# Score products over all 128 rows of the array, keys masked per head, in one core's gated-attention training kernel

## The chip, the cores and the metric

The kernel runs on one core of one Trainium2 chip. The metric is the device time of one execution in microseconds (us); lower is better. One profiled execution gives a trace with every instruction of the engines: PE (TensorE matmul), PEld (TensorE weight load), DVE (VectorE), ACT (ScalarE), POOL (GpSimd) and SP (SyncE, here only a DMA queue). "PEclk" is the TensorE clock that was granted, as a share of full speed; this trace has only the values 0.50 and 1.00 in it, and means between them for longer stretches.

## The reference, cut to what matters

The program computes a gated mix of two attention blocks and all its gradients. Part A is the one that is changed: multi-query attention with 32 query heads of 18 dimensions, one key and one value head, 2048 tokens, no mask.

```
q = (x @ wq).reshape(B, S, 32, 18)          # S = 2048
k = x @ wk ;  v = x @ wv                    # one head of 18
scores = einsum('bhqd,bkd->bhqk', q, k) * 18 ** -0.5
p = softmax(scores) ;  o = einsum('bhqk,bkd->bhqd', p, v)
a = o.reshape(B, S, 32 * 18) @ wo
out = sigmoid(x . gate_w) * a + (1 - sigmoid(x . gate_w)) * b
# reference(): out and its gradients by jax.vjp
```

Part B (`b`, a memory-augmented recurrent attention) and its gradients take the rest of the time and are not touched.

## The kernel before

Part A stands first in the program. `a_setup` loads x and the weights, projects keys and values and writes the queries and the output gradients to memory. `a_attention` is the long part, and the one that the change edits. `a_final` makes the weight gradients. Then Part B runs.

`a_attention` goes over 8 groups of 4 heads. A group's 128 partitions hold 4 heads of 32 rows each; of the 32, 18 are the head's dimensions and one carries an offset, so that 19 are used. `kaug` and `vaugT` hold the one key and value head, repeated for the four places. A group begins with `tr16`, which transposes tiles of 128x128 on PE: two calls make `qtok` and `doT`, and a third, between the two loops, makes `doaT`.

Each group then runs two loops of 4 blocks with 16 iterations each, so 512 iterations of each loop over all groups:

- Loop 1 (for a block of 512 queries, over 16 key tiles) makes the output and the query gradient.
- Loop 2 (for a block of 512 keys, over 16 query tiles) makes the key and value gradients.

An iteration treats the four heads as two pairs. For a pair it computes the scores `s` (two matmuls), the gradient products `d` (two matmuls), the exponential `E = exp(s)` on ACT and `U = d * E` on DVE. E and U then go as moving operand into accumulating matmuls: in loop 1 with `evA`/`evB` (64 columns of the array) and `ku` (32 columns), in loop 2 with `dog` and `qtok` (32 columns each). The matmuls of a pair lie at different row groups (`s`, `d`) or column groups (the others) of the array, given by `tp`, and two that stand next to each other in the instruction order run at the same time. In this text such a stream of 512 columns, of one matmul or of several at the same time, is called a slot.

The two tiles of two PSUM banks, `s` and `d`, come from one pool tag `a_w` of three buffers; the two accumulators take the other two of the eight banks. Instruction order on each engine is set when the program is built, by a scheduler that works from these dependences and buffers; each engine runs its list in order.

In rows of the profile and of the instruction order all matmuls stand at line 66 (`mm`) or 71 (`tr`), so they are told apart by their tiles: `a_w<-a_qaug,a_kaug` is a score product, `a_w<-a_doT,a_vaugT` a gradient product of loop 1 (`a_vaugT,a_doaT` of loop 2), `a_acc<-...` an accumulation. A shape such as `19*128 19x512` means 19 active rows, 128 active columns, and a moving operand of 19 partitions by 512.

Of the kernel before, what the change touches and what calls it, by code (L numbers as in the profile page):

```python
# [6 lines left out]
ACT = mybir.ActivationFunctionType  # L7
ALU = mybir.AluOpType
AX = mybir.AxisListType
BF16 = mybir.dt.bfloat16  # L10
F32 = mybir.dt.float32
P = 128
# [17 lines left out]
class Kern:  # L30
# [1055 lines left out]
    def a_attention(self, keep, sp, pacc, ps):  # L1086


        nc = self.nc
# [5 lines left out]

        def tr16(src_fn, dst):
            for t4 in range(0, NTT, 8):
                pt = ps.tile([P, 8, P], BF16, name="a_w", bufs=3)
                for t in range(8):
                    self.tr(pt[:, t, :], src_fn(t4 + t), P)  # L1100
                self.evac(dst[:, t4 * P:(t4 + 8) * P], pt[:].rearrange("p t c -> p (t c)"))

        for g in range(8):
            qaug = sp.tile([P, T], BF16, name="a_qaug", bufs=2)
# [4 lines left out]
            tr16(lambda t: qaug[:, t * P:(t + 1) * P], qtok)  # L1109
            doT = sp.tile([P, T], BF16, name="a_doT", bufs=1)  # L1110
            tr16(lambda t: dog[:, t, :], doT)
            srows = [slice(32 * i, 32 * i + 19) for i in range(4)]
            for qb in range(T // 512):
                qs = slice(qb * 512, qb * 512 + 512)
                acc = [pacc.tile([P, 512], F32, name=f"a_acc{b}", bufs=1) for b in range(2)]
                for kt in range(NTT):
                    ks = slice(kt * P, (kt + 1) * P)
                    Es, Us = [], []
                    for pr in range(2):
                        s = ps.tile([P, 2, 512], F32, name="a_w", bufs=3)  # L1120
                        for j in range(2):
                            r = srows[2 * pr + j]
                            self.mm(s[:, j, :], lhsT=self.kaug[r, ks], rhs=qaug[r, qs], tp=(r.start, 0))
                        d = ps.tile([P, 2, 512], F32, name="a_w", bufs=3)
                        for j in range(2):
                            r = srows[2 * pr + j]
                            self.mm(d[:, j, :], lhsT=self.vaugT[r, ks], rhs=doT[r, qs], tp=(r.start, 0))
                        ex = sp.tile([P, 2, 512], BF16, name="a_E", bufs=4)
                        nc.scalar.activation(ex[:], s[:], ACT.Exp, scale=SCALEA)  # L1129
                        u = sp.tile([P, 2, 512], BF16, name="a_U", bufs=4)  # L1130
                        nc.vector.tensor_tensor(out=u[:], in0=d[:], in1=ex[:], op=ALU.mult)  # L1131
                        Es.append(ex)
                        Us.append(u)
                    for pr in range(2):
                        ev = self.evA if pr == 0 else self.evB
                        for j in range(2):
                            self.mm(acc[pr][64 * j:64 * j + 64, :], lhsT=ev[:, kt, :], rhs=Es[pr][:, j, :],
                                    start=(kt == 0), stop=False, tp=(0, 64 * j))
                    for pr in range(2):
                        for j in range(2):  # L1140
                            b = 64 * j + (32 if pr == 0 else 0)
                            self.mm(acc[pr][b:b + 32, :], lhsT=self.ku[:, kt, :], rhs=Us[pr][:, j, :],
                                    start=False, stop=(kt == NTT - 1), tp=(0, b))
                accs = sp.tile([P, 2, 512], F32, name="a_accs", bufs=1)
                nc.scalar.copy(accs[:, 0, :], acc[0][:, :])
                nc.vector.tensor_copy(accs[:, 1, :], acc[1][:, :])
                pt = ps.tile([P, 2, 4, P], F32, name="a_w", bufs=3)
                for b in range(2):
                    for t in range(4):
                        nc.tensor.transpose(pt[:, b, t, :], accs[:, b, t * P:(t + 1) * P], self.identF[:])  # L1150
                tk = sp.tile([P, 2, 4, P], F32, name="a_tk", bufs=1)
                nc.scalar.copy(tk[:], pt[:])
                ts = slice(qb * 4, qb * 4 + 4)
                for b in range(2):
                    v = tk[:, b].rearrange("p t (j c) -> p t j c", c=64)
                    o0, k1, k2, u0 = (0, 19, 32, 37) if b == 0 else (32, 51, 0, 5)
                    h0 = 4 * g + 2 * b
                    osl = self.otok[:, ts, h0 * DA:(h0 + 2) * DA].rearrange("p t (j e) -> p t j e", e=DA)
                    qsl = self.dqtok[:, ts, h0 * DA:(h0 + 2) * DA].rearrange("p t (j e) -> p t j e", e=DA)
                    dsl = dog[:, ts, 64 * b:64 * b + 64].rearrange("p t (j c) -> p t j c", c=32)  # L1160
                    rl = sp.tile([P, 4, 2, 1], F32, name="a_rl", bufs=2)
                    nc.vector.reciprocal(rl[:], v[:, :, :, o0 + 18:o0 + 19])
                    nc.gpsimd.tensor_tensor(out=osl, in0=v[:, :, :, o0:o0 + DA], in1=rl[:].to_broadcast([P, 4, 2, DA]),
                                            op=ALU.mult)
                    prod = sp.tile([P, 4, 2, DA], F32, name="a_prod", bufs=2)
                    nc.gpsimd.tensor_tensor(out=prod[:], in0=osl, in1=dsl[:, :, :, 0:DA], op=ALU.mult)
                    dd = sp.tile([P, 4, 2, 1], F32, name="a_dd", bufs=2)
                    nc.vector.tensor_reduce(out=dd[:], in_=prod[:], axis=AX.X, op=ALU.add)
                    m1 = sp.tile([P, 4, 2, DA], F32, name="a_m1", bufs=2)
                    nc.gpsimd.tensor_tensor(out=m1[:, :, :, 0:13], in0=v[:, :, :, k1:k1 + 13],  # L1170
                                            in1=dd[:].to_broadcast([P, 4, 2, 13]), op=ALU.mult)
                    nc.gpsimd.tensor_tensor(out=m1[:, :, :, 13:18], in0=v[:, :, :, k2:k2 + 5],
                                            in1=dd[:].to_broadcast([P, 4, 2, 5]), op=ALU.mult)
                    nc.gpsimd.tensor_tensor(out=m1[:], in0=v[:, :, :, u0:u0 + DA], in1=m1[:], op=ALU.subtract)
                    nc.gpsimd.tensor_tensor(out=dsl[:, :, :, 0:DA], in0=dsl[:, :, :, 0:DA],
                                            in1=rl[:].to_broadcast([P, 4, 2, DA]), op=ALU.mult)
                    nc.vector.scalar_tensor_tensor(out=dsl[:, :, :, DA:DA + 1].rearrange("p t j c -> p t (j c)"),
                                                   in0=dd[:].rearrange("p t j c -> p t (j c)"), scalar=-1.0,
                                                   in1=rl[:].rearrange("p t j c -> p t (j c)"),
                                                   op0=ALU.mult, op1=ALU.mult)  # L1180
                    rls = sp.tile([P, 4, 2, 1], F32, name="a_rls", bufs=2)
                    nc.gpsimd.tensor_scalar(out=rls[:], in0=rl[:], scalar1=SCALEA, scalar2=None, op0=ALU.mult)
                    nc.gpsimd.tensor_tensor(out=qsl, in0=m1[:], in1=rls[:].to_broadcast([P, 4, 2, DA]), op=ALU.mult)
            doaT = sp.tile([P, T], BF16, name="a_doaT", bufs=1)
            tr16(lambda t: dog[:, t, :], doaT)
            for kb in range(T // 512):
                ks = slice(kb * 512, kb * 512 + 512)
                acc = [pacc.tile([P, 512], F32, name=f"a_acc{b}", bufs=1) for b in range(2)]
                for qt in range(NTT):
                    qs = slice(qt * P, (qt + 1) * P)  # L1190
                    Es, Us = [], []
                    for pr in range(2):
                        s = ps.tile([P, 2, 512], F32, name="a_w", bufs=3)
                        for j in range(2):
                            r = srows[2 * pr + j]
                            self.mm(s[:, j, :], lhsT=qaug[r, qs], rhs=self.kaug[r, ks], tp=(r.start, 0))
                        d = ps.tile([P, 2, 512], F32, name="a_w", bufs=3)
                        for j in range(2):
                            r = srows[2 * pr + j]
                            self.mm(d[:, j, :], lhsT=doaT[r, qs], rhs=self.vaugT[r, ks], tp=(r.start, 0))  # L1200
                        ex = sp.tile([P, 2, 512], BF16, name="a_E", bufs=4)
                        nc.scalar.activation(ex[:], s[:], ACT.Exp, scale=SCALEA)  # L1202
                        u = sp.tile([P, 2, 512], BF16, name="a_U", bufs=4)
                        nc.vector.tensor_tensor(out=u[:], in0=d[:], in1=ex[:], op=ALU.mult)  # L1204
                        Es.append(ex)
                        Us.append(u)
                    for b, src, lt in ((0, Es, lambda i: dog[:, qt, 32 * i:32 * i + 32]),
                                       (1, Us, lambda i: qtok[:, qt * P + 32 * i:qt * P + 32 * i + 32])):
                        for i in range(4):
# [223 lines left out]
```

## Time and profile before

| what | value |
|---|---|
| median of 3 runs | 11707.12 us (11702.79 to 11712.66) |
| the profiled execution | 11713.39 us, span of its instructions 11711.6 us |
| PE busy | 10959.3 us, 94% of the span |
| DVE, ACT, POOL busy | 4411.1, 3615.3, 1254.4 us |
| mean granted TensorE clock | 0.722 |
| `a_attention` (first transposition to last accumulation) | 184.45 to 5053.34 us |

The profile cuts the span into 40 equal slices of 293 us; `a_attention` fills slices 1 to 17. Where matmuls are pipelined, a PE that is "busy" need not run at its peak, and at a granted clock of 0.50 the same column count takes twice the time, which counts as busy too. So PE's row has to be read together with the row of the clock.

### The profile page before, as it was taken

To read this page: it belongs to the slowest core of one execution; us is meant where nothing else is said; L and a number is where in the kernel's file an instruction comes from. 1 tells how busy PE (TensorE), PEld (TensorE's weight loads), DVE (VectorE), ACT (ScalarE), POOL (GpSimd) and SP (SyncE) were. 2 spreads that over 40 slices of the span, in tenths; PEclk is the share of its full clock that TensorE was granted. 3 is DMA by queue.
4 is the path that set the end of the run, shared out by engine and by line. 5 is a ranking of instruction groups with operands and counts; after the bars stand their busy time and mean duration, and the time that the engine had idled before them with its cause. 6 is when DMAs were issued, how large, how long until landed. Compare 5 with 4: busy or idle time off the path is not lost. (4 is left out here: it accounts for less than half of the span.)

```text
span 11711.6 us, 208963 instructions
## 1 busy us (share of the span) xinstructions
PE 10959.3 (94%) x91222; PEld 4451.6 (38%) x91222; DVE 4411.1 (38%) x6054; ACT 3615.3 (31%) x4858; POOL 1254.4 (11%) x2894
## 2 busy tenths in 40 slices
PE   7999999999999999989989998888879998999799
PEld 2212121212121212134445555555546665555444
DVE  4555555555555555534422223333322222111200
ACT  3444444444444444423311112222211111111100
POOL 3000000000000000013300002222210000111200
PEclk7555555555555555579989997777779998777799
DMA  2000000000000000035521114444442224666644
GB/s 67 1 4 1 4 1 4 1 4 1 1 4 1 4 1 1 1 116 234 218 82 49 51 49 164 161 155 155 158 164 78 79 78 137 189 189 185 205 144 146
DMA packets 550248, 961.27 MB, mean 82 GB/s; under 512 B 183433, under 2 KB 361746, under 8 KB 529170
## 3 DMA queue, kind: packets, MB, share of 16 engines
q1 hardware_dynamic: 482850, 693.21, 18.5%
q0 software_dynamic: 65168, 253.37, 5.7%
q8 instruction: 713, 11.68, 0.4%
q14 instruction: 205, 1.68, 0.0%
q10 hardware_dynamic: 1312, 1.33, 0.0%
HBM read 543.67 MB, written 404.03 MB: 81 GB/s over the span
## 5 line engine op out<-in xcount | busy, mean ns | idle before, releaser
L1204 DVE TENSOR_TENSOR a_U<-a_w,a_E 128x1024 bf16<-128x1024 f32 x1024 | 1252.0, 1224 | 1131.6 <-ACT a_E L1202 1088.3
L1131 DVE TENSOR_TENSOR a_U<-a_w,a_E 128x1024 bf16<-128x1024 f32 x1024 | 1253.5, 1225 | 964.7 <-ACT a_E L1129 964.7
L1202 ACT ACTIVATE a_E<-a_w 128x1024 bf16<-128x1024 f32 x1024 | 1048.6, 1024 | 1376.8 <-PE a_w L66 1375.5
L1129 ACT ACTIVATE a_E<-a_w 128x1024 bf16<-128x1024 f32 x1024 | 1047.9, 1024 | 1182.7 <-PE a_w L66 1182.7
L66 PE MATMUL a_w<-a_kaug,a_qaug 19*128 19x512 bf16 x2048 | 902.5, 601 | 4.1 <-ACT a_E L1202 3.4
L66 PE MATMUL a_w<-a_vaugT,a_doaT 19*128 19x512 bf16 x2048 | 836.7, 621 | 20.5 <-DVE a_U L1204 14.7
L66 PE MATMUL a_acc<-a_E,a_dog 128*32 128x512 bf16 x2048 | 626.1, 602 | 71.4
L66 PE MATMUL a_w<-a_doT,a_vaugT 19*128 19x512 bf16 x2048 | 671.7, 624 | 4.9 <-ACT a_E L1129 3.8
L66 PE MATMUL a_w<-a_qaug,a_kaug 19*128 19x512 bf16 x2048 | 659.1, 600 | 3.7 <-ACT a_doT L63 3.2
L66 PE MATMUL a_acc<-a_U,a_ku 128*32 128x512 bf16 x2048 | 626.2, 608 | 0.0
L66 PE MATMUL a_acc<-a_U,a_qtok 128*32 128x512 bf16 x2048 | 623.8, 607 | 0.6 <-DVE a_U L1204 0.6
L66 PE MATMUL w_acc<-w_col,w_h 128*128 128x512 bf16 (+1 forms) x2400 | 526.3, 381 | 11.3 <-DMA w_col<-dqx 11.3
L66 PEld LDWEIGHTS <-d_g 128*32 128x32 bf16 x18432 | 498.8, 97 | 30.1 <-issue 11.1
L66 PEld LDWEIGHTS <-a_qaug 19*128 19x128 bf16 x2048 | 152.2, 98 | 655.5 <-issue 655.5
L61 DVE CAST p_tok<-p_pb 128x512 bf16<-128x512 f32 x384 | 265.3, 692 | 318.6 <-PE p_pb L66 318.6
L66 PE MATMUL a_acc<-a_E,a_evB 128*64 128x512 bf16 x1024 | 326.5, 613 | 53.6 <-ACT a_E L1129 0.6
L66 PEld LDWEIGHTS <-a_dog 128*32 128x32 bf16 x2048 | 109.4, 101 | 652.6 <-issue 652.4
L66 PEld LDWEIGHTS <-w_h 128*128 128x128 bf16 (+1 forms) x2400 | 237.5, 101 | 300.3 <-issue 35.1
L66 PEld LDWEIGHTS <-a_ku 128*32 128x32 bf16 x2048 | 105.3, 101 | 640.6 <-issue 640.6
L66 PEld LDWEIGHTS <-a_qtok 128*32 128x32 bf16 x2048 | 107.8, 101 | 623.8 <-issue 623.4
L63 ACT COPY p_em<-p_tr 128x512 bf16<-128x512 bf16 x384 | 225.1, 586 | 357.9 <-PE p_tr L71 356.4
L66 PE MATMUL a_acc<-a_E,a_evA 128*64 128x512 bf16 x1024 | 325.2, 633 | 0.0
(484 smaller groups left out, 15185.9 us busy)
## 6 DMA issues: line engine op xcount, KB each, us to landing
xt_k<-p_tok SPq DMA_DIRECT2D x16, 1024.0 KB, 3.9
xe_k<-p_em POOLq DMA_DIRECT2D x16, 1024.0 KB, 5.3
xs_k<-p_seg POOLq DMA_DIRECT2D x64, 256.0 KB, 3.6
xt_v<-p_tok SPq DMA_DIRECT2D x16, 1024.0 KB, 4.3
xe_v<-p_em POOLq DMA_DIRECT2D x16, 1024.0 KB, 5.7
xs_v<-p_seg POOLq DMA_DIRECT2D x64, 256.0 KB, 3.7
xt_q<-p_tok SPq DMA_DIRECT2D x16, 1024.0 KB, 4.3
xe_q<-p_em POOLq DMA_DIRECT2D x16, 1024.0 KB, 5.7
```

The lines of the kernel that those rows point to most:

```text
L61: nc.vector.tensor_copy(out, in_)
L63: nc.scalar.copy(out, in_)
L66: return self.nc.tensor.matmul(out, lhsT, rhs, start=start, stop=stop, tile_position=tp, skip_group_check=True)
L1129: nc.scalar.activation(ex[:], s[:], ACT.Exp, scale=SCALEA)
L1131: nc.vector.tensor_tensor(out=u[:], in0=d[:], in1=ex[:], op=ALU.mult)
L1202: nc.scalar.activation(ex[:], s[:], ACT.Exp, scale=SCALEA)
L1204: nc.vector.tensor_tensor(out=u[:], in0=d[:], in1=ex[:], op=ALU.mult)
```

## The change

The change edits `a_attention` alone. The score product of a head no longer uses the head's own 32 rows, but all 128: the queries (all four heads of the group) stand against `kmask`, a copy of the keys with one slice per head in which the rows of the other three heads are zero. `kmask` is filled at the start of `a_attention`: a memset on POOL and four copies on DVE. The score matmul has no row group any more (no `tp`), so two of them can't run at the same time. The gradient products keep their row groups, but now take 32 rows instead of 19 (the rest are zero). Scores go to tiles of one bank (`a_s`, two buffers) and their exponential is made per head, in two instructions of 512 instead of one of 1024. The gradient products keep two banks (`a_d`, two buffers). Together that is again six banks.

```diff
+        srows = [slice(32 * i, 32 * i + 32) for i in range(4)]
+        kmask = keep.tile([P, 4, T], BF16, name="a_kmask")
+        nc.gpsimd.memset(kmask[:], 0.0)
+        for i in range(4):
+            nc.vector.tensor_copy(kmask[srows[i], i, :], self.kaug[srows[i], :])
+
+        def pair(pr, sl, sr, dl, dr):
+
+            d = ps.tile([P, 2, 512], F32, name="a_d", bufs=2)
+            ex = sp.tile([P, 2, 512], BF16, name="a_E", bufs=4)
+            for j in range(2):
+                s = ps.tile([P, 512], F32, name="a_s", bufs=2)
+                self.mm(s[:, :], lhsT=sl(2 * pr + j), rhs=sr(2 * pr + j))
+                nc.scalar.activation(ex[:, j, :], s[:, :], ACT.Exp, scale=SCALEA)
+            for j in range(2):
+                r = srows[2 * pr + j]
+                self.mm(d[:, j, :], lhsT=dl(r), rhs=dr(r), tp=(r.start, 0))
+            u = sp.tile([P, 2, 512], BF16, name="a_U", bufs=4)
+            nc.vector.tensor_tensor(out=u[:], in0=d[:], in1=ex[:], op=ALU.mult)
+            return ex, u
...
-            srows = [slice(32 * i, 32 * i + 19) for i in range(4)]
...
-                    for pr in range(2):
-                        s = ps.tile([P, 2, 512], F32, name="a_w", bufs=3)
-                        for j in range(2):
-                            r = srows[2 * pr + j]
-                            self.mm(s[:, j, :], lhsT=self.kaug[r, ks], rhs=qaug[r, qs], tp=(r.start, 0))
-                        d = ps.tile([P, 2, 512], F32, name="a_w", bufs=3)
...
+                    Es, Us = zip(*[pair(pr, lambda i: kmask[:, i, ks], lambda i: qaug[:, qs],
+                                        lambda r: self.vaugT[r, ks], lambda r: doT[r, qs]) for pr in range(2)])
...
+                    Es, Us = zip(*[pair(pr, lambda i: qaug[:, qs], lambda i: kmask[:, i, ks],
+                                        lambda r: doaT[r, qs], lambda r: self.vaugT[r, ks]) for pr in range(2)])
```

The second pair of lines is loop 2, where the queries are the stationary and the masked keys the moving operand. The other uses of `a_w` (the transpositions) move to `a_d`.

The edit also changes the instruction order. On PE in the middle of a block of loop 1, before, a pair's two score matmuls stand together, then its two gradient matmuls, then the two with `evA`:

```order
L66 LDWEIGHTS a_kaug
L66 MATMUL a_w<-a_qaug,a_kaug 128x512 [waits PE_49]
L66 LDWEIGHTS a_kaug
L66 MATMUL a_w<-a_qaug,a_kaug 128x512
L66 LDWEIGHTS a_vaugT
L66 MATMUL a_w<-a_doT,a_vaugT 128x512 [waits Activation_49]
L66 LDWEIGHTS a_vaugT
L66 MATMUL a_w<-a_doT,a_vaugT 128x512
L66 LDWEIGHTS a_evA
L66 MATMUL a_acc_19185<-a_E,a_evA 64x512
L66 LDWEIGHTS a_evA
L66 MATMUL a_acc_19185<-a_E,a_evA 64x512
```

At the same place now, each score matmul stands alone between matmuls of other forms, and the pair with `evA` is taken apart:

```order
L66 LDWEIGHTS a_kmask
L66 MATMUL a_s<-a_qaug,a_kmask 128x512 [waits Activation_49]
L66 LDWEIGHTS a_evA
L66 MATMUL a_acc_21431<-a_E,a_evA 64x512
L66 LDWEIGHTS a_ku
L66 MATMUL a_acc_21432<-a_U,a_ku 32x512 [waits DVE_49]
L66 LDWEIGHTS a_ku
L66 MATMUL a_acc_21432<-a_U,a_ku 32x512
L66 LDWEIGHTS a_kmask
L66 MATMUL a_s<-a_qaug,a_kmask 128x512 [waits Activation_49]
L66 LDWEIGHTS a_vaugT
L66 MATMUL a_d<-a_doT,a_vaugT 128x512 [waits PE_49]
```

A whole iteration of loop 1 is now, in slots (A and B are the two pairs): score A1, gradient pair A, score B0, evA0, ku pair of B, score B1, gradient pair B, evA1 with evB0, evB1, score of the next A0, ku pair of A: eleven slots, where eight stood before (two score pairs, two gradient pairs, evA pair, evB pair, two ku pairs).

On PE in the middle of a block of loop 2, before, one score pair is split by the pair with `qtok`:

```order
L66 LDWEIGHTS a_qaug
L66 MATMUL a_w<-a_kaug,a_qaug 128x512 [waits PE_49]
L66 LDWEIGHTS a_qtok
L66 MATMUL a_acc_5623<-a_U,a_qtok 32x512 [waits DVE_49]
L66 LDWEIGHTS a_qtok
L66 MATMUL a_acc_5623<-a_U,a_qtok 32x512
L66 LDWEIGHTS a_qaug
L66 MATMUL a_w<-a_kaug,a_qaug 128x512
L66 LDWEIGHTS a_doaT
L66 MATMUL a_w<-a_vaugT,a_doaT 128x512
```

Now two of the four score matmuls follow each other, and the `dog` matmuls of a pair stand apart:

```order
L66 LDWEIGHTS a_doaT
L66 MATMUL a_d<-a_vaugT,a_doaT 128x512 [waits PE_49]
L66 LDWEIGHTS a_doaT
L66 MATMUL a_d<-a_vaugT,a_doaT 128x512
L66 LDWEIGHTS a_dog
L66 MATMUL a_acc_6076<-a_E,a_dog 32x512 [waits Activation_49]
L66 LDWEIGHTS a_qaug
L66 MATMUL a_s<-a_kmask,a_qaug 128x512
L66 LDWEIGHTS a_qaug
L66 MATMUL a_s<-a_kmask,a_qaug 128x512 [waits Activation_49]
L66 LDWEIGHTS a_dog
L66 MATMUL a_acc_6076<-a_E,a_dog 32x512
```

A whole iteration of loop 2 is now: score A1, score B0, dog A0 with the qtok pair of B, gradient pair A, score B1, dog A1 with dog B0, score of the next A0, qtok pair of A, gradient pair B, dog B1: ten slots.

On POOL at the start of `a_attention` the memset of `kmask` stands ahead of the loads of `dog` of the first two groups, which POOL's queue issues:

```order
L1081 MEMSET a_dos 128x1024 [waits DMAHW1_49,Activation_49]
L1105 MEMSET a_kmask 128x8192 [waits DMAHW3_49,DMAHW4_49,DMAHW2_49,DMAHW6_49,DVE_49,Activation_49]
L1128 DMA a_dog<-do_dram 128x2048 [waits DMASW6_49]
L1128 DMA a_dog<-do_dram 128x2048 [waits DMASW7_49]
L1169 TENSOR_TENSOR a_otok<-a_tk,a_rl 128x4x36 [waits DVE_49]
```

Before, the first of these loads stood there in the memset's place.

More of the change, by code (lines that the diff above doesn't have):

```diff
@@ L1097, in tr16 @@
             for t4 in range(0, NTT, 8):
-                pt = ps.tile([P, 8, P], BF16, name="a_w", bufs=3)
+                pt = ps.tile([P, 8, P], BF16, name="a_d", bufs=2)
                 for t in range(8):
@@ L1117, in a_attention @@
                     ks = slice(kt * P, (kt + 1) * P)
-                    Es, Us = [], []
-                    for pr in range(2):
-                        s = ps.tile([P, 2, 512], F32, name="a_w", bufs=3)
-                        for j in range(2):
-                            r = srows[2 * pr + j]
-                            self.mm(s[:, j, :], lhsT=self.kaug[r, ks], rhs=qaug[r, qs], tp=(r.start, 0))
-                        d = ps.tile([P, 2, 512], F32, name="a_w", bufs=3)
[L1125 to L1133, printed above, removed]
+                    Es, Us = zip(*[pair(pr, lambda i: kmask[:, i, ks], lambda i: qaug[:, qs],
+                                        lambda r: self.vaugT[r, ks], lambda r: doT[r, qs]) for pr in range(2)])
                     for pr in range(2):
@@ L1146, in a_attention @@
                 nc.vector.tensor_copy(accs[:, 1, :], acc[1][:, :])
-                pt = ps.tile([P, 2, 4, P], F32, name="a_w", bufs=3)
+                pt = ps.tile([P, 2, 4, P], F32, name="a_d", bufs=2)
                 for b in range(2):
@@ L1190, in a_attention @@
                     qs = slice(qt * P, (qt + 1) * P)
[L1191 to L1206, printed above, removed]
+                    Es, Us = zip(*[pair(pr, lambda i: qaug[:, qs], lambda i: kmask[:, i, ks],
+                                        lambda r: doaT[r, qs], lambda r: self.vaugT[r, ks]) for pr in range(2)])
                     for b, src, lt in ((0, Es, lambda i: dog[:, qt, 32 * i:32 * i + 32]),
```

## Prediction

> **What bounds the kernel now.** I read the page first, for the share of each engine and the clock in 40 slices (the digits are tenths):
>
> ```profile
> PE 10959.3 (94%) x91222; PEld 4451.6 (38%) x91222; DVE 4411.1 (38%) x6054; ACT 3615.3 (31%) x4858; POOL 1254.4 (11%) x2894
> PE   7999999999999999989989998888879998999799
> PEclk7555555555555555579989997777779998777799
> ```
>
> PE is full in slices 1 to 17, which are `a_attention`, and there its clock is at half. Then the table of stretches, with the whole of `a_attention` first and two stretches of Part B under it:
>
> ```profile
> core 0: us, PE busy (x) PEld busy (x) DVE busy (x) ACT busy (x) POOL busy (x), PEclk, DMA share, GB/s
> 184.45:5053.34 4868.89, 4685.68 (x17024) 969.57 (x17025) 2621.46 (x2355) 2169.74 (x2140) 181.26 (x518) 0.50 0.01 2
> 5250.00:5800.00 550.00, 550.00 (x3276) 232.09 (x3276) 251.53 (x364) 213.36 (x364) 209.44 (x289) 1.00 0.58 231
> 6000.00:7000.00 1000.00, 996.30 (x16638) 502.73 (x16638) 232.60 (x558) 197.05 (x391) 29.29 (x112) 1.00 0.16 49
> L66 PE MATMUL c_S<-Wo,c_mE 128*32 128x192 bf16 x5280 | 155.1, 246 | 0.0
> ```
>
> `a_attention` takes 4868.9 us, bound by PE (96% busy) at half clock; DVE needs 2621 and ACT 2170. Other stages, no busier, run at 1.00, and the last row shows that they may use few columns (32) as long as they use 128 rows. So being busy doesn't give the clock. To see what does, the timeline of one iteration of loop 1 (evA to evA, 4.34 us) and loop 2 (dog to dog, 4.84 us):
>
> ```profile
> 1501.86 0.64 PE L66 MATMUL a_acc<-a_E,a_evA 128*64 128x512 bf16 x2
> 1502.62 0.64 PE L66 MATMUL a_acc<-a_E,a_evB 128*64 128x512 bf16 x2
> 1503.18 0.61 PE L66 MATMUL a_acc<-a_U,a_ku 128*32 128x512 bf16 x2
> 1503.73 0.61 PE L66 MATMUL a_w<-a_qaug,a_kaug 19*128 19x512 bf16 x2
> 1504.13 0.63 PE L66 MATMUL a_w<-a_doT,a_vaugT 19*128 19x512 bf16 x2
> 1504.38 1.02 ACT L1129 ACTIVATE a_E<-a_w 128x1024 bf16<-128x1024 f32 x1 [1.81 <-PE a_w L66]
> 1504.69 0.61 PE L66 MATMUL a_acc<-a_U,a_ku 128*32 128x512 bf16 x2
> 1505.23 0.61 PE L66 MATMUL a_w<-a_qaug,a_kaug 19*128 19x512 bf16 x2
> ...
> 1506.20 0.64 PE L66 MATMUL a_acc<-a_E,a_evA 128*64 128x512 bf16 x2
> ...
> 700.32 1.37 PE L66 MATMUL a_acc<-a_E,a_dog 128*32 128x512 bf16 x4
> ...
> 705.16 1.37 PE L66 MATMUL a_acc<-a_E,a_dog 128*32 128x512 bf16 x4
> ```
>
> Half of loop 1's eight slots use 2x19 = 38 of 128 rows, so weighted by rows there stream 4 + 4x0.30 = 5.2 slots. One slot is 0.43 us at half clock (transpositions of 128 columns, below, start every 0.107 us; 512 columns are four times that). So 2.22 of 4.34 us are filled with rows: a share of 0.51. Now the one kind of place where the loops do get the clock, the transpositions at a group's start (three stretches, then what PE ran in the first of them):
>
> ```profile
> 794.22:797.63 3.41, 3.41 (x26) 2.34 (x26) 1.31 (x3) 0.92 (x2) 0.34 (x1) 0.50 0.56 189
> 797.63:801.05 3.42, 2.23 (x18) 0.93 (x17) 1.60 (x2) 3.40 (x4) 0.00 (x0) 1.00 0.00 0
> 801.05:804.46 3.41, 3.38 (x12) 0.70 (x13) 1.50 (x3) 1.02 (x1) 0.00 (x0) 0.50 0.00 0
> 794.12 0.61 PE L66 MATMUL a_acc<-a_U,a_qtok 128*32 128x512 bf16 x2
> 794.66 1.46 PE L71 MATMUL a_w<-identB,a_qaug 128*128 128x128 bf16 x12
> 796.05 0.61 PE L66 MATMUL a_acc<-a_U,a_qtok 128*32 128x512 bf16 x2
> 796.60 1.21 PE L71 MATMUL a_w<-identB,a_dog 128*128 128x128 bf16 x10
> ```
>
> The first stretch holds 22x0.107 + 0.33 + 0.43 = 3.1 us of slots on all 128 rows: a share of 0.9, no busier than the loops, and the next 3.41 us run at full clock. In these the score pairs with 38 rows return, and the clock falls back.
>
> I worked out this row share for all 3431 stretches of 3.41 us in the trace, from each matmul's start, rows and columns (row groups at the same time add up, column groups count once, f32 twice, full clock doubles the columns). A limit of 0.725 tells the next stretch's clock wrong in 10 of them; rows times columns, at its best limit, in 29; streaming of any width in 69. That limit is the step on which the forecast rests.
>
> By the Trainium skill (TensorE: Matmul & The Clock Gate, Part 1) a monitor of how busy PE has been, in windows of some 3.4 us, opens the clock; by busy time alone the loops here would be at full clock. The trace disagrees with that reading, with 0.50 at 96% busy.
>
> **The change, part by part.** First the price of a change of form between slots. At half clock, from the rows above: ku to scores 0.55 us, gradients to ku 0.56, evB to ku 0.56, against 0.43 for the columns, so 0.11 to 0.13 more; within one form (scores to gradients) 0.40, nothing more. At full clock, in one of the few stretches:
>
> ```profile
> 2018.10 0.39 PE L66 MATMUL a_w<-a_doT,a_vaugT 19*128 19x512 bf16 x2 [0.54 <-ACT a_E L1129]
> 2018.42 0.41 PE L66 MATMUL a_acc<-a_E,a_evA 128*64 128x512 bf16 x2
> 2019.02 0.41 PE L66 MATMUL a_acc<-a_E,a_evB 128*64 128x512 bf16 x2 [0.19 <-ACT a_E L1129]
> 2019.36 0.40 PE L66 MATMUL a_w<-a_qaug,a_kaug 19*128 19x512 bf16 x1
> 2019.68 0.61 PE L66 MATMUL a_acc<-a_U,a_ku 128*32 128x512 bf16 x2
> ```
>
> Slots of 0.32, 0.34, 0.32, against 0.21 of columns: the price stays 0.11 us whatever the clock. A change from an all-rows matmul to a row group isn't in the trace; I take 0.11 too, between 0.09 and 0.13.
>
> *Scores alone.* Loop 1 goes from 8 to 11 slots with 10 changes of form, loop 2 to 10 slots with 9. At half clock: 11x0.427 + 10x0.11 = 5.80 us (from 4.34) and 10x0.427 + 9x0.11 = 5.26 (from 4.84). At full clock: 11x0.213 + 1.10 = 3.44 and 10x0.213 + 0.99 = 3.12.
>
> *The row share.* Loop 1 has 9 slots on all rows and two gradient pairs of 38: 9.6x0.427 = 4.10 us of 5.80, a share of 0.71 already at half clock, at the limit; and 2x9.6x0.213/3.65 = 1.12 at full clock. Loop 2: 8.6 slots, 0.70 and 1.16. So half clock is left as soon as a stretch comes out a little over the mean or at the next transposition, and full clock is kept with much to spare. That the rows multiply zeros shouldn't matter: in the transpositions the moving operand is an identity, nearly all zeros, and counts. Taking 32 rows instead of 19 in the gradients costs no columns.
>
> *Exponentials in halves.* ACT rows and DVE's:
>
> ```profile
> L812 ACT ACTIVATE g_dt<-x_p 128x512 bf16<-128x512 f32 x256 | 142.8, 599 | 355.1 <-DMA dvx<-g_dt 192.1 <-PE x_p L66 161.7 <-issue 1.3
> L1131 DVE TENSOR_TENSOR a_U<-a_w,a_E 128x1024 bf16<-128x1024 f32 x1020 | 1248.7, 1225 | 960.3 <-ACT a_E L1129 960.3
> ```
>
> Four of 0.60 are 2.4 us and two products of 1.225 are 2.45, both under 3.1: hidden by PE, with some 0.7 us to spare in loop 2. But evB1 waits for the last exponential. A score slot reaches ACT 0.22 us after its columns (1504.38 less 1503.73 less 0.43), so at full clock 0.21 + 0.22 + 0.60 + 0.05 = 1.08 us after score B1's start; PE has slots of 0.32, 0.32 and 0.21 between, 0.85. That is a wait of 0.2: loop 1 takes 3.65. In loop 2 the score matmuls run further ahead; I add 0.05: 3.17. Bounds: no wait, or 0.5 us (two one-bank buffers turn out too few).
>
> *kmask.* Its memset stands before the loads of `dog` in POOL's queue:
>
> ```profile
> L970 POOL MEMSET a_wqp<- 128x5120 bf16 x1 | 4.4, 4383 | 0.0
> 186.59 1.89 PE L71 MATMUL a_w<-identB,a_dog 128*128 128x128 bf16 x16 [0.27 <-DMA a_dog<-do_dram]
> ```
>
> 8192 columns at 4.38/5120 are 7.0 us by which the load, for which PE waited at 186.59, comes later; the four copies on DVE (0 to 2 us each) mostly lie beside it. I put +8 us, once, between 5 and 15.
>
> *Sum.* 512x(3.65 + 3.17) = 3492 against 512x(4.34 + 4.84) = 4700: -1208. Another 169 us of `a_attention` (4869 - 4700) lie at the turns of blocks, where PE is at half clock as well; between nothing and half of it goes, and I take the half, -84, since these are the same slots. With +8: -1284. The span 11711.6 becomes 10,428; that execution took 11713.4 in all, and the median of the runs, 11707.1, stands 4.5 under its span: 10,423. I add 17 for stretches at half clock after the drops at a block's turn (3.41 us at half speed lose about 1.7, ten such): 10,440. The rest of the program is untouched. Own range: 19 changes of form x512x0.02 is 195 each way, waits of 0.3 more 150 to 300, a loop pass of 64 iterations caught at half clock 64x2.1 = 135: 10,290 to 10,800.
>
> **The rivals.**
>
> *The clock stays at half.* The limit is misread: the monitor doesn't count rows that hold zeros, or the share at half clock, 0.71, stays under and each grant is lost again, as after 801.05 now. The place is the same eleven and ten slots, the price 512x(5.80 + 5.26) = 5663, so +963, and with +8 about 12,680. It decides where a stretch at full clock in the new loops shows a share under 0.72; worked out it is 1.12. For it: the share at half clock is right at the limit. Against it: 10 misses in 3431, and the transpositions.
>
> The Trainium skill speaks for it (TensorE: Matmul & The Clock Gate, Why this matters for your kernels): for small K it advises row groups, since matmuls in them run at the same time, and K=32 takes as long alone as K=128. By that alone the three and more slots added are a loss, and the sum is this rival's; the trace agrees on the pairs (two scores in 0.40 us).
>
> *Only one loop keeps the clock.* Say loop 2, with fewer slots on all rows, falls back at its start, where PE waits for the first exponentials (797.63 to 801.05: PE busy 2.23 of 3.42), and stays at half: 512x(3.65 + 5.26) = 4562, -138, with turns and kmask about 11,540. The other way round 512x(5.80 + 3.17) = 4593: about 11,580.
>
> *ACT or DVE become the bound.* At 2.4 and 2.45 us per iteration they'd hold PE only if their rows lengthened by 0.7 us; it would give at most the waits already in the range.
>
> **How the numbers follow.** Full clock nearly throughout 0.77; only one loop, or half of the passes, 0.11; half clock 0.12. The time is that of the first, 10,440. Its own range holds 0.74; up to 11,300, which takes in a third to a half of the passes caught at half clock, about 0.79. A measurement of this kernel tells 0.2% (23 us) from no change. Faster by more: 0.77 + 0.10 = 0.87; slower: 0.12; within: 0.01.
>
> **What would show it.** Right: slices of `a_attention` at 9 or 10 tenths in PEclk; an iteration of loop 1 at 3.65 us and of loop 2 at 3.17; score rows `a_s` alone, with 128*128; slots of 0.32 us between forms; evB1 waiting on ACT for 0.2 us; the first score some 8 us later. Wrong: PEclk at 5, slots of 0.54 and iterations of 5.8 and 5.3 us (the limit), or full clock with idle PE before `a_s` or `a_d` (buffers).

## The result and the profile after

The changed kernel takes 10,380.8 us (median of 4 runs, 10,379.9 to 10,382.7) against 11,705.0 us (4 runs, 11,701.6 to 11,712.7): a ratio of 0.8868, with a 95% interval of 0.8853 to 0.8883. The forecast was 10,440 us, with 10,290 to 10,800 as the range of its likeliest case and 11,300 as the outer end; the likeliest case came.

The page after, in its rows for PE and for the clock (40 slices, now of 259 us; `a_attention` fills slices 1 to 14), and two of its groups of instructions:

```profile
PE 9786.8 (94%) x91222; PEld 4483.1 (43%) x91222; DVE 4400.1 (42%) x6058; ACT 3878.9 (37%) x6906; POOL 1258.1 (12%) x2895
PE   7999999999999989979999888888799989999899
PEclk9999999999999999979999877777899997777899
...
L1121 DVE TENSOR_TENSOR a_U<-a_d,a_E 128x1024 bf16<-128x1024 f32 x2048 | 2498.0, 1224 | 851.0 <-PE a_d L66 367.5
L1116 ACT ACTIVATE a_E<-a_s 128x512 bf16<-128x512 f32 x4096 | 2369.8, 597 | 1075.4 <-PE a_s L66 919.6
```

PE is as busy as before, 94%, and has the same number of matmuls; what differs is the clock's row, which had 5 in slices 1 to 16 and now has 9. The table of stretches gives `a_attention` in one row (columns as in the prediction):

```profile
184.98:3734.67 3549.69, 3519.92 (x17024) 1005.47 (x17025) 2612.46 (x2359) 2435.23 (x4188) 185.47 (x521) 0.99 0.01 3
```

It takes 3549.7 us instead of 4868.9 us, at a mean clock of 0.99. Of 1041 stretches of 3.41 us, 14 are at half clock. Now an iteration of loop 1 on PE, from evB at 705.63 to evB at 709.28, with the exponential on ACT that the prediction said PE would wait for:

```profile
705.31 0.39 PE L66 MATMUL a_d<-a_doT,a_vaugT 32*128 32x512 bf16 x2
705.41 0.60 ACT L1116 ACTIVATE a_E<-a_s 128x512 bf16<-128x512 f32 x1 [0.38 <-PE a_s L66]
705.63 0.40 PE L66 MATMUL a_acc<-a_E,a_evA 128*64 128x512 bf16 x1
705.63 0.81 PE L66 MATMUL a_acc<-a_E,a_evB 128*64 128x512 bf16 x2
706.37 0.39 PE L66 MATMUL a_s<-a_qaug,a_kmask 128*128 128x512 bf16 x1
706.69 0.39 PE L66 MATMUL a_acc<-a_U,a_ku 128*32 128x512 bf16 x2
707.01 0.39 PE L66 MATMUL a_s<-a_qaug,a_kmask 128*128 128x512 bf16 x1
707.34 0.39 PE L66 MATMUL a_d<-a_doT,a_vaugT 32*128 32x512 bf16 x2
...
709.28 0.40 PE L66 MATMUL a_acc<-a_E,a_evB 128*64 128x512 bf16 x1
```

Slots of different forms follow each other every 0.32 us, from all-rows scores to the gradient pair too (707.01 to 707.34). The last exponential runs from 705.41 to 706.01, and the second evB matmul ends at 706.44, so it began at about 706.05: 0.2 us later than its turn. The iteration is 3.65 us. Loop 2, from dog to dog:

```profile
495.33 0.39 PE L66 MATMUL a_acc<-a_E,a_dog 128*32 128x512 bf16 x1
495.33 0.39 PE L66 MATMUL a_acc<-a_U,a_qtok 128*32 128x512 bf16 x2
495.66 0.39 PE L66 MATMUL a_d<-a_vaugT,a_doaT 32*128 32x512 bf16 x2
495.98 0.39 PE L66 MATMUL a_s<-a_kmask,a_qaug 128*128 128x512 bf16 x1
496.30 0.43 PE L66 MATMUL a_acc<-a_E,a_dog 128*32 128x512 bf16 x2
...
497.95 0.60 PE L66 MATMUL a_s<-a_kmask,a_qaug 128*128 128x512 bf16 x2
498.49 0.39 PE L66 MATMUL a_acc<-a_E,a_dog 128*32 128x512 bf16 x1
```

That is 3.16 us, for ten slots with nine changes of form.

### The profile page after: what moved, and what is told of

Same layout as the page of the kernel before. It is cut to its first block, busy times and chain, and to the rows that moved or that the text cites. A ratio compares the mean times of both kernels' runs of the same rounds, so it can differ in the third digit from the quotient of the medians.

```text
span 10378.1 us, 211015 instructions
## 1 busy us (share of the span) xinstructions
PE 9786.8 (94%) x91222; PEld 4483.1 (43%) x91222; DVE 4400.1 (42%) x6058; ACT 3878.9 (37%) x6906; POOL 1258.1 (12%) x2895
## 5 line engine op out<-in xcount | busy, mean ns | idle before, releaser
L1121 DVE TENSOR_TENSOR a_U<-a_d,a_E 128x1024 bf16<-128x1024 f32 x2048 | 2498.0, 1224 | 851.0 <-PE a_d L66 367.5
L1116 ACT ACTIVATE a_E<-a_s 128x512 bf16<-128x512 f32 x4096 | 2369.8, 597 | 1075.4 <-PE a_s L66 919.6
L66 PE MATMUL a_s<-a_qaug,a_kmask 128*128 128x512 bf16 x2048 | 783.3, 392 | 3.2 <-DVE a_kmask L1107 2.0
L66 PE MATMUL a_s<-a_kmask,a_qaug 128*128 128x512 bf16 x2048 | 719.3, 387 | 1.5
L66 PEld LDWEIGHTS <-a_kmask 128*128 128x128 bf16 x2048 | 183.5, 96 | 567.5 <-issue 564.2
L66 PE MATMUL a_d<-a_doT,a_vaugT 32*128 32x512 bf16 x2048 | 409.5, 388 | 3.3 <-ACT a_doT L63 2.4
L66 PE MATMUL a_acc<-a_U,a_ku 128*32 128x512 bf16 x2048 | 405.9, 393 | 4.2 <-DVE a_U L1121 4.1
L66 PE MATMUL a_d<-a_vaugT,a_doaT 32*128 32x512 bf16 x2048 | 400.5, 384 | 4.9 <-DVE a_U L1121 4.9
L66 PE MATMUL a_acc<-a_U,a_qtok 128*32 128x512 bf16 x2048 | 402.3, 389 | 1.2 <-DVE a_U L1121 1.2
L66 PEld LDWEIGHTS <-c_mT 128*32 128x32 bf16 (+1 forms) x7680 | 166.8, 94 | 330.6 <-issue 211.7
```

The lines of the kernel that those rows point to most:

```text
L66: return self.nc.tensor.matmul(out, lhsT, rhs, start=start, stop=stop, tile_position=tp, skip_group_check=True)
L1116: nc.scalar.activation(ex[:, j, :], s[:, :], ACT.Exp, scale=SCALEA)
```

## Which part of the change brings the time: experiments

The theory is the prediction's: the clock of a stretch of 3.41 us follows the share of rows that streamed in the stretch before. The rivals: the one-bank tiles, the half exponentials and the new order take waits away; or the 32 rows of the gradient products matter; or only a matmul that uses all 128 rows by itself counts.

**The new tiles and order without the rows.** The score products of the changed kernel go back to a row group each. On PE the instruction order is that of the changed kernel, but for some matmuls in the first iterations; `kmask` is still filled, but nobody reads it.

```diff
-                self.mm(s[:, :], lhsT=sl(2 * pr + j), rhs=sr(2 * pr + j))
+                r = srows[2 * pr + j]
+                self.mm(s[:, :], lhsT=sl(r), rhs=sr(r), tp=(r.start, 0))
...
-   pair(pr, lambda i: kmask[:, i, ks], lambda i: qaug[:, qs], ...
+   pair(pr, lambda r: self.kaug[r, ks], lambda r: qaug[r, qs], ...
```

> The changed kernel, but each score product takes only its head's own 32 rows again (a row group of kaug and qaug, no kmask); one-bank score tiles, exponentials in halves and the instruction order on PE stay as they are. Theory (the granted clock follows the share of rows that stream): a score slot fills 32 of 128 rows, so loop 1 has 5 slots on all rows, 4 of a quarter and 2 of a half, 7 x 0.427 = 3.0 us in an iteration of about 4.9 us at half clock (scores beside gradient products have the same form and partly run at the same time), a share of 0.61; loop 2 is alike with 4.8 us. Both under 0.725: PEclk in a_attention 0.50, a_attention 5050 to 5170 us, the program 11,880 to 12,010 us, slower than before. Rival (the tiles, the half exponentials and the order bring the gain): iterations of 3.3 to 3.6 us and 3.1 us, the program at about 10,300 to 10,400 us.

Measured: 11,954.0 us in one run, beside 11,707.8 us for the kernel before. Its row of the table of stretches for `a_attention`, and then four rows of the timeline of loop 1:

```profile
184.04:5300.10 5116.06, 5101.56 (x17024) 972.52 (x17025) 2621.32 (x2359) 2401.78 (x4188) 185.29 (x521) 0.51 0.01 2
```

```profile
899.94 0.64 PE L66 MATMUL a_acc<-a_E,a_evA 128*64 128x512 bf16 x1
900.51 0.61 PE L66 MATMUL a_acc<-a_U,a_ku 128*32 128x512 bf16 x2
901.05 0.60 PE L66 MATMUL a_s<-a_qaug,a_kaug 32*128 32x512 bf16 x1
901.05 1.03 PE L66 MATMUL a_d<-a_doT,a_vaugT 32*128 32x512 bf16 x2
```

PE is busy for 5101.6 of 5116.1 us, 99.7%, at a clock of 0.51, and slots are 0.54 to 0.57 us apart. Tiles, exponentials and order alone make the kernel slower: the score pairs that ran as one slot are taken apart, and nothing pays for it. The first rival falls.

**The rows without the new tiles.** The kernel before, with `kmask` and its score products on all rows; two-bank tiles, three buffers, whole exponentials and (but for the first iterations) the order stay. As in the change, the gradient products take 32 rows here.

```diff
+        srows = [slice(32 * i, 32 * i + 32) for i in range(4)]
...
-            srows = [slice(32 * i, 32 * i + 19) for i in range(4)]
...
-   self.mm(s[:, j, :], lhsT=self.kaug[r, ks], rhs=qaug[r, qs], tp=(r.start, 0))
+   self.mm(s[:, j, :], lhsT=kmask[:, 2 * pr + j, ks], rhs=qaug[:, qs])
...
-   self.mm(s[:, j, :], lhsT=qaug[r, qs], rhs=self.kaug[r, ks], tp=(r.start, 0))
+   self.mm(s[:, j, :], lhsT=qaug[:, qs], rhs=kmask[:, 2 * pr + j, ks])
```

> The kernel before, with its two-bank tiles, three buffers and whole exponentials, and only the score products on all 128 rows against kmask. Theory (row share): loop 1 has 8 slots on all rows and two gradient pairs of 38 of 128, 8.6 x 0.427 = 3.67 us in 5.1 to 5.3 us at half clock, 0.69 to 0.72, and far over the limit once at full clock; so it gets and keeps full clock like the changed kernel: iterations of about 3.6 us (a pair's scores, exponential and product in one chain through three buffers), a_attention 3800 to 4000 us, the program 10,650 to 10,850 us. Rival (tiles and order bring the gain, rows don't count): half clock, 10 slots, 5.3 us in both loops, the program at about 12,450 us.

Measured: 10,709.1 us in one run, beside the same 11,707.8. The row for `a_attention`, and two of the timeline of its loop 1, where the bracket gives idle time and its releaser:

```profile
182.50:4061.61 3879.11, 3349.91 (x17024) 948.89 (x17025) 2576.34 (x2359) 2166.14 (x2140) 185.31 (x521) 0.98 0.01 3
```

```profile
899.65 0.41 PE L66 MATMUL a_acc<-a_E,a_evA 128*64 128x512 bf16 x2
900.51 0.41 PE L66 MATMUL a_acc<-a_E,a_evB 128*64 128x512 bf16 x2 [0.45 <-ACT a_E L1134]
```

The rows alone bring 999 us of the change's 1324. With them the clock is 0.98; then PE is fast enough to wait 0.45 us in an iteration of loop 1 for the whole exponential of the second pair, where the changed kernel waits 0.2 us for a half one. So the tiles and the order are worth 328 us more (10,709 to 10,381), but only at full clock: at half clock they cost 251 us (11,703 of the next kernel to 11,954).

**32 rows instead of 19, in the kernel before.** One line: `srows` takes 32 rows for scores and gradients.

```diff
-            srows = [slice(32 * i, 32 * i + 19) for i in range(4)]
+            srows = [slice(32 * i, 32 * i + 32) for i in range(4)]
```

> The kernel before with 32 instead of 19 rows in all score and gradient products (the added rows are zeros). Theory (row share): 4 + 4 x 0.5 = 6 slots, 2.56 us of 4.34 us, a share of 0.59, still under 0.725: half clock, the time as before within 0.3 per cent (11,670 to 11,740 us). Rival (the gradient products on 32 rows are what brings the clock, or whole 32-row groups count as full): full clock, 10,400 us or less.

Measured: 11,702.6 us in one run, beside 11,707.8; `a_attention` takes 4864.6 us (row of the table of stretches):

```profile
183.05:5047.64 4864.59, 4677.55 (x17024) 967.88 (x17025) 2620.01 (x2355) 2167.67 (x2140) 180.81 (x518) 0.51 0.01 2
```

A share of 0.59 in loop 1 (an estimate: six of eight slots' worth of rows, 2.56 of 4.34 us) is not enough, and nothing changes. Rows that cost no columns, and bring no share over the limit, are worth nothing.

**The kernel before with pairs that fill the array.** Each score and gradient product takes 64 rows: heads 0 and 2 form a pair, and heads 1 and 3; `kmask` and a like `vmask` hold keys and values with the other head's rows zero within each half. Two products of a pair still run at the same time, at rows 0 and 64. Tiles and columns are those of before, and so is the order on PE but for some matmuls in the first iterations.

```diff
+        half = [slice(0, 64), slice(64, 128)]
...
-   r = srows[2 * pr + j]
-   self.mm(s[:, j, :], lhsT=self.kaug[r, ks], rhs=qaug[r, qs], tp=(r.start, 0))
+   r = half[j]
+   self.mm(s[:, j, :], lhsT=kmask[r, pr, ks], rhs=qaug[r, qs], tp=(r.start, 0))
```

> The kernel before, its two-bank tiles, whole exponentials and, but for sixteen matmuls in the first iterations, its instruction order on PE; only the score and gradient products take 64 rows each instead of 19 (heads 0 and 2, heads 1 and 3 as pairs, keys and values masked within 64 rows, rows 0 and 64), so a pair fills all 128. The number of matmuls and their columns are those of before. Theory (row share): all 8 slots are on all rows, 8 x 0.427 = 3.42 us of 4.34 us (loop 1) and of 4.84 us (loop 2), 0.79 and 0.71 at half clock, so loop 1 leaves half clock by itself; at full clock 1.0, kept in both. Then the chain of a pair (scores, exponential 1.02 us, product 1.22 us) through three buffers sets the pace, 3.2 us and 3.4 us, and a_attention takes 3550 to 3650 us, the program 10,390 to 10,490 us. Rival (one-bank tiles, half exponentials or the new order are needed for the gain): half clock or not, 4.3 us and 4.8 us stay, 11,700 us.

Measured: 10,391.8 us (10,381.0 to 10,394.2, 4 runs), a ratio of 0.8877, interval 0.8863 to 0.8890: the same as the whole change, with as many matmuls and columns as before and none of the change's tiles or order. The row for `a_attention`, and three of loop 1's timeline:

```profile
183.54:3739.66 3556.12, 2989.33 (x17024) 884.04 (x17025) 2536.13 (x2363) 2090.54 (x2140) 185.77 (x521) 0.99 0.01 3
```

```profile
715.97 0.39 PE L66 MATMUL a_acc<-a_U,a_ku 128*32 128x512 bf16 x2 [0.19 <-DVE a_U L1139]
...
717.00 0.41 PE L66 MATMUL a_acc<-a_E,a_evA 128*64 128x512 bf16 x2
717.80 0.41 PE L66 MATMUL a_acc<-a_E,a_evB 128*64 128x512 bf16 x2 [0.40 <-ACT a_E L1137]
```

PE is busy only 84% here (2989 of 3556 us) and waits for DVE and ACT; in the steady part of a block an iteration of loop 1 takes 3.09 and 3.30 us in turn, one of loop 2 takes 3.38. The less busy PE has the full clock and the fuller one of the first experiment (99.7%) has half. By the Trainium skill (TensorE: Matmul & The Clock Gate, Why this matters for your kernels) products of small K are to be put in row groups so that they run together. The runs show where that advice holds here: groups of 64 rows that fill the array keep both the overlap and the clock (0.99), pairs of 19 or 32 rows that leave rows empty lose the clock (0.50 and 0.51).

**More work, less time.** The slow kernel of the first experiment, with sixteen extra matmuls on all 128 rows at the head of each block, 1024 in all, whose result nobody reads.

```diff
+   kick = ps.tile([P, 2, 512], F32, name="a_d", bufs=2)
+   for i in range(16):
+       self.mm(kick[:, i % 2, :], lhsT=self.kaug[:, 0:P], rhs=qaug[:, 0:512])
```

> The kernel with scores on their own 32 rows in the changed kernel's order (it took 11,954 us, half clock), with 16 more matmuls of 512 columns on all 128 rows at the head of each of the 64 blocks, into a tile that nobody reads: 1024 matmuls of pure extra work. Theory (row share with a limit that is the same for getting and for keeping the clock, since it counts columns in 3.41 us): the 16 fill a stretch and bring full clock; at full clock the loops fill 7 x 0.427 = 3.0 us in about 3.3 us, a share of 0.9, and keep it until a block's turn. Iterations 3.4 us and 3.1 us, a_attention 3620 to 3750 us with the 64 x 3.5 us of the extra work, the program 10,460 to 10,590 us, over 1,300 us faster by more work. Rival (the share of rows has to be high in itself, or only matmuls on all rows hold the clock): it falls back to half a stretch or two after each burst, a_attention 5300 us or more, the program 12,100 to 12,300 us.

Measured: 10,527.4 us in one run, 1427 us less than without the extra work. `a_attention` takes 3690 us. From the table of stretches, two of them, each of 32 us, in the first and second block of loop 1 of the fifth group:

```profile
2100.00:2132.00 32.00, 31.78 (x102) 7.24 (x103) 14.17 (x12) 14.12 (x26) 0.00 (x0) 0.50 0.00 1
2140.00:2172.00 32.00, 30.80 (x152) 6.92 (x151) 22.52 (x19) 21.71 (x39) 0.00 (x0) 1.00 0.01 2
```

It is the same loop at two speeds, with 102 and 152 matmuls in 32 us. At the start of five groups a stretch with a share of 0.61 to 0.73 lets the clock fall (here at 2057.2); at half clock the loop fills 0.55 to 0.63 and stays there, 5.1 us an iteration, for the block's whole 75 us; the next block's burst fills a stretch, and from 2132.3 the same loop fills 0.9 and holds full clock at 3.4 us an iteration until the next fall. So one limit on the row share decides both over getting and over keeping the clock, and a loop that could keep it may never reach it by itself.

**The gradient products of the changed kernel on 19 rows again.** Nothing else is changed.

```diff
-                r = srows[2 * pr + j]
+                r = slice(32 * (2 * pr + j), 32 * (2 * pr + j) + 19)
                 self.mm(d[:, j, :], lhsT=dl(r), rhs=dr(r), tp=(r.start, 0))
```

> The changed kernel with 19 instead of 32 rows in the gradient products, nothing else. Theory (row share): at full clock nothing changes; at half clock the share goes from 10 x 0.427 / 5.8 = 0.74 to 9.6 x 0.427 / 5.8 = 0.71, under the limit of 0.725 on the mean, so each drop at a block's turn lasts longer: between 5 and 70 us slower, 10,385 to 10,450 us, with more stretches at half clock than the 14 of the changed kernel. Rival (rows of the gradient products don't count): 10,375 to 10,385 us with the same stretches.

Measured: 10,436.7 us in one run, 56 us more than the changed kernel. From the same table, two stretches of 50 us of the fourth group, in the first and the second block of its loop 1:

```profile
1540.00:1590.00 50.00, 48.59 (x137) 9.65 (x139) 20.82 (x17) 19.68 (x34) 0.00 (x0) 0.50 0.00 0
1610.00:1660.00 50.00, 48.74 (x220) 13.79 (x223) 34.13 (x29) 33.09 (x56) 1.27 (x4) 1.00 0.00 1
```

Two of the 32 blocks of loop 1 run at half clock. The fourth group's takes 82.8 us from its first to its last ku product (1519.2 to 1602.0), where the same block of the changed kernel takes 51.4, so the two lose 63 us. That is the prediction's first rival in small. Once the clock has fallen, this loop hovers under the limit (shares of 0.54 to 0.74 for 80 us); with 32 rows a like fall in the changed kernel, at 3290.2, ends after eight stretches, when one reaches 0.757. The changed kernel's own two falls cost some 15 us, so `a_attention` is 47 us longer here (3597.2 us after 3549.7), and the other 9 of the 56 us lie in the untouched rest. The 13 rows of zeros per product are worth those 47 us, in one run with two falls. That they count shows in the stretches as well: with 32 in the place of the 19 rows, the row share tells the clock wrong in 14 stretches of this run, and with 19 in 2. The rival that they don't count falls.

**Both together.** The changed kernel's tiles with the pairs on 64 rows, for scores and gradients.

```diff
-   self.mm(s[:, :], lhsT=sl(2 * pr + j), rhs=sr(2 * pr + j))
+   r = half[j]
+   self.mm(s[:, :], lhsT=sl(pr, r), rhs=sr(pr, r), tp=(r.start, 0))
```

> The changed kernel's tiles, with score and gradient products on 64 rows each: heads 0 and 2, and heads 1 and 3, form the pairs, keys and values are masked within 64 rows, and the two products of a pair stand at rows 0 and 64, so that together they use all 128 rows and can run at the same time. Theory (row share): all slots are on all rows or come in pairs that are, where the order keeps the pair together; with full clock there are two to three slots fewer than in the changed kernel, iterations of about 3.3 us in loop 1 and 2.55 us in loop 2 (DVE's two products of 1.22 us become the bound there), a_attention 3080 to 3150 us, the program 9,920 to 9,980 us. Where a score stands alone in its slot it fills only half of the rows; if that puts one loop under the limit at half clock, that loop stays at 4.5 us or 3.6 us and the program ends at 10,380 to 10,700 us. Rival (a score must use all 128 rows by itself): half clock in both loops, a_attention about 4290 us, the program 11,120 us.

Measured: 10,290.2 us in one run, in neither of the two ranges. The direction was right, the size wrong: iterations take 3.41 and 3.15 us in the steady part of a block, and loop 2, for which I had expected 2.55 us and DVE as the bound, is the larger miss. Whether this kernel beats the changed one takes more than one run:

> The kernel with products on 64 rows in the changed kernel's tiles, as run once before at 10,290 us, now timed: 10,280 to 10,310 us, a ratio to before of 0.879.

Measured: 10,282.2 us (10,280.9 to 10,293.4, 4 runs), a ratio of 0.8788 to the kernel before, interval 0.8773 to 0.8802, under that of the change (0.8853 to 0.8883): some 98 us faster than it. The row for `a_attention`, and an iteration of loop 2:

```profile
182.64:3632.48 3449.84, 3355.80 (x17024) 854.44 (x17025) 2617.90 (x2363) 2378.44 (x4188) 185.78 (x521) 0.99 0.01 3
```

```profile
935.09 0.39 PE L66 MATMUL a_d<-a_vmask,a_doaT 64*128 64x512 bf16 x2
935.51 0.37 PE L66 MATMUL a_s<-a_kmask,a_qaug 64*128 64x512 bf16 x1
935.82 0.56 PE L66 MATMUL a_acc<-a_E,a_dog 128*32 128x512 bf16 x2
936.31 0.39 PE L66 MATMUL a_s<-a_kmask,a_qaug 64*128 64x512 bf16 x1
936.62 0.39 PE L66 MATMUL a_acc<-a_U,a_qtok 128*32 128x512 bf16 x2
936.95 0.39 PE L66 MATMUL a_d<-a_vmask,a_doaT 64*128 64x512 bf16 x2
937.27 0.39 PE L66 MATMUL a_acc<-a_E,a_dog 128*32 128x512 bf16 x1
937.59 0.39 PE L66 MATMUL a_s<-a_kmask,a_qaug 64*128 64x512 bf16 x2
937.91 0.39 PE L66 MATMUL a_acc<-a_E,a_dog 128*32 128x512 bf16 x1
937.91 0.39 PE L66 MATMUL a_acc<-a_U,a_qtok 128*32 128x512 bf16 x2
```

PE is the bound again (97% busy), and most slots of 0.21 us of columns still cost some 0.32, since the order alternates the forms. One of the two score pairs runs together (937.59); the other is taken apart (935.51 and 936.31), so nine slots are left of the changed kernel's ten.

The four corners side by side, in us of the program: old tiles with few rows 11,708, new tiles with few rows 11,954, old tiles with all rows 10,709 (or 10,392 in pairs of 64), new tiles with all rows 10,381 (10,282 in pairs). The 11,954 and the 10,709 are single runs.

Over the ten traces (before, after and eight runs of experiments) I worked the row share out for the 11,733 stretches of `a_attention`, as in the prediction. One limit for all, 0.75, tells the next stretch's clock wrong in 24; streaming of any width, at its best limit, in 126, and rows times columns in 197. The clock changes some 150 times in these stretches, so a rule that it stays as it is would be wrong that often, and streaming of any width tells hardly more than that. Two stretches show what parts the counts (full clock doubles the columns, so a share can pass 1): the one at 529.0 of the first experiment streams 1.17 in any width but 0.70 in rows, and the clock falls; the one at 1401.8 of the kernel before streams 0.78 in both, and the clock rises.

## Why the prediction was right, point by point

- *The bound and the clock.* Right: in all nine kernels the clock went as the row share said, whatever the tiles, the order and the busy time. The limit of 0.725, fixed before any of these runs, was a little low: 34 of the 11,733 stretches are wrong by it, and 24 by 0.75, which is fitted to them. One step to it was misread: the stages of Part B that I called no busier are busier by their rows, 100% and 99.6% against 96%, so they did not show that being busy doesn't give the clock. The first experiment (99.7% busy, 0.51) and the pairs of 64 rows (84%, 0.99) do.
- *Shares at half clock, 0.71 and 0.70.* Too low by a slip: I took 38 of 128 rows for the gradient pairs, though I had written that they take 32 rows each, 64 together, now. With those it is 10 x 0.427 / 5.80 = 0.74 in loop 1 and 9 x 0.427 / 5.26 = 0.73 in loop 2. I called the 13 rows free of charge; they are, but not without worth, as the 47 us without them show. The chance of half clock, 0.12, rested on the lower share.
- *Slots and changes of form.* Right: 0.32 us a slot at full clock, from all rows to a row group too. By the Trainium skill (TensorEngine Tiling (Array Packing), Key Properties) a change of tiling mode drains the array; the rows here put the price of a change of form at 0.11 us at full clock, and at 0.11 to 0.14 at half (slots of 0.54 to 0.57 us in the first experiment).
- *The iterations, 3.65 and 3.17 us.* Measured 3.65, with the wait of 0.2 us at the second evB, and 3.16. By these iterations of the steady part of a block, the sum of 3492 us for 1024 of them stands at 512 x (3.65 + 3.16) = 3487.
- *Turns of blocks, -84, kmask +8, half-clock stretches +17.* These three were mis-sized together. They left 85 + 8 + 17 = 110 us of `a_attention` outside of the iterations; measured are 3549.7 - 3487 = 63 us. 14 stretches at half clock were forecast as ten.
- *kmask.* The memset takes 6.92 us (7.0 forecast), and POOL issues the loads of `dog` 7.2 us later than before (187.99 after 180.78). But the rest of the step failed: "the first score some 8 us later" was 0.4 us, since the scores don't need `dog`.

```profile
181.12 6.92 POOL L1105 MEMSET a_kmask<- 128x8192 bf16 x1 [3.31 <-DMA do_dram<-a_dos]
187.99 1.61 POOL L1128 DMA_DIRECT2D a_dog<-do_dram  x2
188.81 1.32 PE L66 MATMUL a_s<-a_qaug,a_kmask 128*128 128x512 bf16 x2 [1.97 <-DVE a_kmask L1107]
193.25 1.55 PE L71 MATMUL a_d<-identB,a_dog 128*128 128x128 bf16 x16
```

  The transpositions of `dog` came 6.7 us later than at 186.59 before, and in front of them PE ran the first five scores, which it had to do anyway. The first block's iterations take 3.8 us instead of 3.5 us in most other groups' first blocks, some 4 us in all, so the price was about half of the eight, and part of it is the clock's.
- *The rest of the program, untouched.* It took 6643.4 us after `a_attention`'s end, where it was 6658.3: 15 us less, with no edit there. Over the other traces that rest is between 6645.7 and 6654.0, so it wanders by some us; why is not shown, and I don't count it for the change.
- *ACT and DVE.* Right that they stay behind PE: 2435 and 2612 us of 3550.

The total of 10,440 was 59 us too high: 47 from turns and kmask, 15 from the rest and 5 from the iterations, less 7 because the median now stands 2.7 us over the profiled span, where it stood 4.5 under it.

## What to carry to other kernels

When PE is busy all the time and the clock's row says half, count rows, not time: a stream that fills 38 of 128 partitions counts as 0.3 of one. Fill the array at no cost in columns, best with row groups that together use all 128 rows and still run at the same time, before touching tiles or order; what a saved wait is worth depends on the clock, and may turn its sign. A loop whose share lies near the limit needs a margin at half clock, or a short burst of full rows, to come back after each turn.

## What was new about the hardware

- The same loop can hold either clock: it ran 75 us long at half clock (shares of 0.55 to 0.63) and hundreds of us at full clock (0.9), and the burst that switched it is sixteen matmuls, 3.4 to 6.8 us of columns.
- PE at 99.7% busy had a clock of 0.51, and PE at 84% busy had 0.99.
- Rows that hold zeros counted: three quarters of `kmask` and 13 of 32 gradient rows are zeros. Whether a matmul with nothing but zeros counts was not tried, and why rows and not columns are counted stays open.
